# The first 336 columns of w_o as two loads of their own, one of them read in 5 groups of 16 rows

## The chip, the cores and the metric

The kernel runs on one core of one Trainium2 chip. The metric is the device time of one execution in microseconds (us), lower is better. The core has a matmul engine (PE), a vector engine (DVE), a scalar engine (ACT), a general one (POOL) and one that issues most transfers (SP). Transfers (DMAs) between the chip's memory (HBM) and the on-chip buffer (SBUF, 128 partitions) are carried out by 16 DMA engines, which are fed from queues: q1 holds what SP issues, q10 what ACT issues.

## What is computed

A decode step with one new token for each of two sequences. The input is normalised; one branch is attention over a cache of 4096 keys and values (16 query heads, 8 key heads, head size 256), followed by the output projection `wo`; the other is a small gated feed-forward. Cut to what matters:

```
xn = layernorm(x)                                  # 2 x 448
q  = xn @ wq                                       # 2 x 16 heads x 256
p  = softmax(q . k_cache / 16)                     # 4096 positions
o  = p . v_cache                                   # 2 x 16 x 256
s  = o.reshape(2, 4096) @ wo                       # wo: 4096 x 448
g  = silu(((xn @ w_gate) * (xn @ w_up)) @ w_down)
out = x + s * g
```

All data are float32. Nearly all bytes are the two caches (64 MB each) and the weights, 158.54 MB of reads, each read once.

## The kernel before

**Work and stages.** The 16 pairs of a key head and a sequence are taken one after the other. For each, PE multiplies the query with the keys (`scores`, tile `s`), DVE and ACT make the softmax, PE turns the weights (`turn`) and multiplies them with the values (`values`, tile `o`), and a few small instructions join the result into `oT`. Ahead of this stand the feed-forward and the query projection, behind it the output projection with `wo`.

**Transfers.** `dma_side` is the whole list of SP's loads in order: `wgu` in two pieces, `wd`, `wq`, then 16 steps of keys and values (`kv`, 8 MB each but for the first step, into the buffers `buf0` and `buf1` in turn), the values of the last two steps (`vv`, two loads of 4 MB), and `wo` in six loads. SP waits before a load only until the buffer it writes is free; so the loads stand in the queue well ahead of their start. ACT issues only two small loads, `x` (2 rows) and `xo` (8 rows).

**The output projection.** `wo` is laid out as 128 rows of 32 steps of 448 columns, one matmul step for each. `ABREAST = (14, 9, 4)` are the steps of the first three loads into the tile `low` (`early` = 27 steps), `DIRECT = (3, 1, 1)` those of the last three into the upper half of `buf1` (`late`). Each load has a semaphore of its own (`won`). In `pe_side`, the loop over `won` waits for a load and then does its steps: those of `low` are summed in four column groups of the tile `o` (`abreast`, line 322), which ACT then copies to `ys` and `spread` (line 326) adds to `acc`; those of `late` go into `acc` directly (line 446). After the last step DVE multiplies with the gate (line 295), adds `x` (line 298), and SP stores the result (line 140).

The part of `dma_side` that the change touches stands on lines 131 to 138; the matmul steps are on lines 433 to 456.

Of the kernel before, what the change touches and what calls it, by code (L numbers as in the profile page):

```python
# [8 lines left out]
B, D = 2, 448  # L9
# [15 lines left out]
WO = 4 * HKV  # L25
ABREAST = (14, 9, 4)
DIRECT = (3, 1, 1)


class Queue:  # L30
# [20 lines left out]
        self.e.wait_ge(sem, n).then_inc(sem, -n)  # L51


def program(nc, known, x, xo, wgu, wd, wq, kv, vv, wo, out):
    def sb(name, shape):
        return nc.alloc_sbuf_tensor(name, shape, F32).ap()

    def ps(name, shape):
        return nc.alloc_psum_tensor(name, shape, F32).ap()

    first = nc.alloc_semaphore("first")
    sems = {n: nc.alloc_semaphore(n) for n in (
        "x", "xg", "gu", "wd", "wq", "k0", "k1", "v14", "v15", "t0", "t1", "pt", "sr", "ob", "q", "m", "mx", "res")}
    won = [nc.alloc_semaphore(f"wo{i}") for i in range(len(ABREAST + DIRECT))]
    pe = Queue(nc, nc.tensor, "pe", known)
    dv = Queue(nc, nc.vector, "dv", known)
# [6 lines left out]
    low = sb("low", [128, 28 * FC])  # L73
# [7 lines left out]
    xg, gate, sig, r0, r1 = (sb(n, [128, SL]) for n in ("xg", "gate", "sig", "r0", "r1"))  # L81
# [8 lines left out]
    m = sb("m", [128, 2])  # L90
    mx = sb("mx", [1, NT, W])
    p = sb("p", [128, 2, 512])
    su = sb("su", [128, 2])
    sr = sb("sr", [128, 128])
    r = [sb(f"r{i}i", [128, REP]) for i in range(2)]
    pT = sb("pT", [128, 2, BLK, 128])
    ob = sb("ob", [128, 512])
# [4 lines left out]
    pt = [ps(f"pt{i}", [128, NK, 128]) for i in range(2)]  # L102
# [4 lines left out]
    late = buf[1][:, ROW:]  # L107
    bounds = [0]
    for n in ABREAST + DIRECT:
        bounds.append(bounds[-1] + n)  # L110
    early = bounds[len(ABREAST)]

    def wo_step(i):
        return low[:, i * D:(i + 1) * D] if i < early else late[:, (i - early) * D:(i - early + 1) * D]
# [4 lines left out]
    def dma_side():  # L119
        e = nc.sync  # L120
        for lo, hi in zip(GU, GU[1:]):
            e.dma_start(low[:, lo:hi], wgu[:, lo:hi]).then_inc(sems["gu"], 16)
        e.dma_start(buf[1][:, :14 * D], wd).then_inc(sems["wd"], 16)
        e.dma_start(buf[0][:, :28 * 512], wq).then_inc(sems["wq"], 16)
        sp.after(pe, "y4")
        for h in range(2):
            e.dma_start(buf[1][:, h * ROW:(h + 1) * ROW], kv[0][:, h * ROW:(h + 1) * ROW]).then_inc(sems[f"k{h}"], 16)
        for i in range(N - 2):
            sp.after(pe, *(("q", 1) if i == 0 else ("s", 1) if i == 1 else ("v", i - 2)))
            e.dma_start(buf[i % 2], kv[1 + i]).then_inc(turns[i % 2], 16)  # L130
        sp.after(pe, "v", N - 4)
        for h in range(2):
            e.dma_start(buf[0][:, h * ROW:(h + 1) * ROW], vv[h]).then_inc(sems[f"v{N - 2 + h}"], 16)
        for n, lo, hi in zip(won, bounds, bounds[1:]):
            if lo == early:
                sp.after(pe, "v", N - 3)
            t = low[:, lo * D:hi * D] if hi <= early else late[:, (lo - early) * D:(hi - early) * D]
            e.dma_start(t, wo[:, lo * D:hi * D]).then_inc(n, 16)
        sp.after(dv, "res")
        e.dma_start(out, r1).then_inc(sems["res"], 16)  # L140
        e.wait_ge(sems["res"], 16)
        last = nc.alloc_semaphore("last")
        e.sem_clear(range(first.num, last.num + 1))
# [156 lines left out]
    def pe_side():  # L300
        e = nc.tensor
# [18 lines left out]
        def abreast(t, lhs, rhs, i, total):  # L320
            c = i % NT
            return e.matmul(t[W * c:W * (c + 1), :D], lhs, rhs, start=i < NT, stop=i >= total - NT)  # L322

        def spread(start, stop):
            for c in range(NT):
                ins = e.matmul(acc[W * c:W * (c + 1), :SL], pick.rearrange("p b j -> p (b j)"),  # L326
                               ys[:, c * SL:(c + 1) * SL], start=start, stop=stop)
            return ins
# [77 lines left out]
        at, count = dict(pe.at), pe.n  # L406
# [26 lines left out]
        def left(i):  # L433
            g, j = divmod(i, 4)
            return oT[g][:, j // 2, j % 2].rearrange("p b j -> p (b j)")

        for n, lo, hi in zip(won, bounds, bounds[1:]):
            e.wait_ge(n, 16)
            for i in range(lo, hi):
                if i >= 4 * (HKV - 1):  # L440
                    pe.after(dv, "oT", N - 1)
                if i < early:
                    ins = abreast(o, left(i), wo_step(i), i, early)
                else:
                    for c in range(NT):
                        ins = e.matmul(acc[W * c:W * (c + 1), :SL], left(i), wo_step(i)[:, c * SL:(c + 1) * SL],  # L446
                                       start=lo == early and i == lo, stop=i == WO - 1)
            if hi == early:
                pe.ev(ins, "w4")
            if lo == early:  # L450
                pe.after(ac, "accs")
                spread(False, False)
# [3 lines left out]
    act_side()  # L456
    dve_side()
    dma_side()
    pe_side()
    return {q.name: q.at for q in (pe, dv, ac, po, sp)}  # L460

# [44 lines left out]
```

## Time and profile before

| | us |
|---|---|
| median of 3 runs | 375.0 (374.96 to 375.05) |
| the profiled execution, its own time | 375.17 |
| its span (first to last instruction of the profile) | 373.9 |

| engine | busy us | share of the span |
|---|---|---|
| PE, matmul | 243.6 | 65% |
| PE, weight load | 95.1 | 25% |
| DVE | 60.3 | 16% |
| ACT | 45.7 | 12% |
| POOL | 5.0 | 1% |
| q1 on the 16 DMA engines | | 98.4% |

The span starts with the first instruction in the profile; the own time also holds the start and the end around it, 1.3 us. The busy share of the DMA engines is a mean over 16: a share of 0.50 in a short stretch can mean that 8 of them are at work and 8 have run out.

### The profile page before, as it was taken

The numbers are of one execution on the slowest core, as the hardware profiler recorded it, in microseconds if no ns is written. First come the engines' busy times: TensorE is split into PE (matmuls) and PEld (weight loads), VectorE is DVE, ScalarE is ACT, GpSimd is POOL, SyncE is SP. The second block draws the span as 40 slices with busy tenths as digits, with TensorE's granted clock in tenths as the row PEclk, the third lists the DMA queues.
The fourth block names the chain that finished last, engine by engine and source line by source line (L and its number), as shares of the span: only waits on it lengthen the run. The fifth ranks groups of instructions, "written<-read, shape, count | busy, mean of one in ns | idle before, by whom it ended". The sixth has DMA issues, their size and how long they took to land. (4 is left out here: it accounts for less than half of the span.)

```text
span 373.9 us, 3749 instructions
## 1 busy us (share of the span) xinstructions
PE 243.6 (65%) x1642; PEld 95.1 (25%) x1642; DVE 60.3 (16%) x142; ACT 45.7 (12%) x105; POOL 5.0 (1%) x23
## 2 busy tenths in 40 slices
PE   0093295739393948585776767575758484849786
PEld 0021022322322222323231313122322222232332
DVE  3001002202121212112021203030302020202100
ACT  1002021010102020202020202020202010201110
POOL 1000000000000000000000000000000000000000
PEclk9998588758677687768596859596959586958899
DMA  9999999999999999999999999999999999999995
GB/s 369 400 459 413 430 424 438 444 444 449 449 429 400 435 429 435 449 442 436 407 435 435 435 442 435 449 428 414 435 428 442 442 442 442 400 417 435 417 421 211
DMA packets 4203, 158.70 MB, mean 424 GB/s; under 512 B 610, under 2 KB 868, under 8 KB 1252
## 3 DMA queue, kind: packets, MB, share of 16 engines
q1 hardware_dynamic: 4176, 158.59, 98.4%
q8 instruction: 5, 0.08, 0.1%
q14 instruction: 2, 0.02, 0.0%
q10 hardware_dynamic: 20, 0.01, 0.0%
HBM read 158.54 MB, written 0.06 MB: 424 GB/s over the span
## 5 line engine op out<-in xcount | busy, mean ns | idle before, releaser
L361 PE MATMUL s<-buf,qs 128*32 128x512 f32 x512 | 89.2, 860 | 58.1 <-PEq L51 58.1
L386 PE MATMUL o<-buf,pT 128*32 128x512 f32 x512 | 76.9, 610 | 0.3 <-DVE oT L272 0.3
L178 ACT ACTIVATE p<-s,m 128x512 f32<-128x512 f32 x32 | 21.7, 682 | 251.6 <-DVE m L253 251.6
L361 PEld LDWEIGHTS s<-buf,qs 128*32 128x32 f32 x512 | 22.5, 151 | 111.2 <-issue 111.1
L247 DVE TENSOR_REDUCE m<-s 128x1 f32<-128x1024 f32 x16 | 19.6, 1224 | 144.8 <-PE s L361 144.8
L317 PE MATMUL pt<-ident,p 128*128 128x128 f32 x128 | 22.2, 329 | 12.8 <-PEq L51 12.8
L394 PE MATMUL oc<-sel,ob 128*128 128x2 f32 x128 | 16.4, 250 | 19.8 <-PEq L51 19.8
L386 PEld LDWEIGHTS o<-buf,pT 128*32 128x32 f32 x512 | 17.1, 111 | 32.9 <-issue 30.6
L394 PEld LDWEIGHTS oc<-sel,ob 128*128 128x128 f32 x128 | 15.5, 191 | 33.9 <-issue 33.9
L317 PEld LDWEIGHTS pt<-ident,p 128*128 128x128 f32 x128 | 17.4, 166 | 13.7 <-issue 13.7
L308 PE MATMUL s<-buf,xnT 128*32 128x512 f32 x48 | 7.9, 813 | 10.8 <-DMA buf<-wq 10.8
L308 PE MATMUL s<-low,xnT 128*32 128x448 f32 x48 | 6.5, 692 | 11.9 <-DMA low<-wgu 11.9
L266 DVE COPY pT<-pt 128x512 f32<-128x512 f32 x16 | 11.1, 691 | 18.3 <-PE o L386 17.0
L249 DVE TENSOR_REDUCE mx<-sm 1x128 f32<-1x512 f32 x16 | 10.9, 679 | 10.1 <-PE sm L367 10.1
L192 ACT COPY ob<-o 128x512 f32<-128x512 f32 x16 | 9.3, 582 | 12.5 <-PE o L386 12.5
L183 ACT COPY pT<-pt 128x512 f32<-128x512 f32 x16 | 9.6, 601 | 2.4 <-PE pt L317 2.4
L371 PEld LDWEIGHTS sm<-one,mx 1*128 1x128 f32 x32 | 4.7, 183 | 13.8 <-issue 13.8
L158 POOL COPY qs<-qT 128x64 f32<-128x64 f32 x16 | 3.7, 236 | 293.8 <-PE s L361 243.1
L377 PEld LDWEIGHTS sm<-sel,sr 128*128 128x128 f32 x32 | 7.4, 288 | 0.0
L371 PE MATMUL sm<-one,mx 1*128 1x1 f32 x32 | 6.0, 255 | 1.7 <-PEq L51 1.7
L322 PE MATMUL o<-low,oT 128*32 128x448 f32 x54 | 6.4, 544 | 0.6 <-DMA low<-wo 0.6
L178 ACT ACTIVATION_READ_ACCUMULATOR p<-s,m 128x1 f32 x32 | 6.3, 196 | 0.0
(65 smaller groups left out, 62.4 us busy)
## 6 DMA issues: line engine op xcount, KB each, us to landing
buf<-kv SPq DMA_DIRECT2D x2, 4096.0 KB, 26.1
buf<-vv SPq DMA_DIRECT2D x2, 4096.0 KB, 23.1
buf<-wq SPq DMA_DIRECT2D x1, 7168.0 KB, 41.9
low<-wgu SPq DMA_DIRECT2D x1, 5824.0 KB, 17.0
buf<-wd SPq DMA_DIRECT2D x1, 3136.0 KB, 24.0
low<-wo SPq DMA_DIRECT2D x1, 3136.0 KB, 34.8
low<-wo SPq DMA_DIRECT2D x1, 2016.0 KB, 39.1
low<-wo SPq DMA_DIRECT2D x1, 896.0 KB, 40.9
```

The costliest lines, as they stand in the source:

```text
L178: ins = e.activation(p[:, h], s[:, h], AF.Exp, bias=m[:, 1:2], scale=1.0 / 16, accum_out=su[:, h:h + 1])
L183: e.copy(pT[:, 1], pt[1]).then_inc(sems["pt"], 1)
L192: e.copy(ob, o).then_inc(sems["ob"], 1)
L247: e.tensor_reduce(m[:, 0:1], s.rearrange("p h n -> p (h n)"), axis=AX.X, op=OP.max).then_inc(sems["m"], 1)
L249: e.tensor_reduce(mx, sm[:1, None, :128].rearrange("p o (c j) -> p o j c", c=NT).to_broadcast([1, NT, W, NT]), axis=AX.X, op=OP.max).then_ ...
L266: e.tensor_copy(pT[:, 0], pt[0]).then_inc(sems["pt"], 1)
L308: e.matmul(t[W * c:W * (c + 1), :n], xnT[:, k, :], block(NT * k + c), start=k == 0, stop=False)
L317: ins = e.transpose(t[:, i, :], a[:, i * 128:(i + 1) * 128], ident)
L361: ins = e.matmul(s[W * c:W * (c + 1), h], qs[i % 2][:, d].rearrange("p j q -> p (j q)"), k[:, h, d, c, :], start=d == 0, stop=d == 1)
L371: pe.ev(e.matmul(sm[:, 128:129], mx.rearrange("p c j -> p (c j)"), one, start=True, stop=True), "x", i)
L386: ins = e.matmul(o[W * at:W * (at + 1), :], pT[:, h, j, 64 * c + 16:64 * c + 48], v[:, h, j, c, :], start=h == 0 and j < 2, stop=h == 1 an ...
L394: ins = e.matmul(oc[:, 2 * d:2 * d + 2], ob[:, h * 256 + d * 128:h * 256 + (d + 1) * 128], sel[:, h], start=h == 0, stop=h == 1)
```

## The change

The first 336 of the first load's 6272 columns are taken out of it and loaded ahead of it in two loads, which share a new semaphore `lead`:

- rows 0 to 79 from a new input array `few`, a copy of that block of `wo` made on the host, stored as 5 groups of 17 rows of which 16 are read. The unused 17th row keeps the 5 groups apart in the access pattern: it is 5 x 16 x 336 in HBM, against 80 rows in SBUF.
- rows 80 to 127 from `wo`, 48 rows of 336 columns.

The first load of `wo` then begins at column 336 and is 128 rows of 5936 columns. Before the first step of the output projection PE waits for `lead` too. All bytes land where they landed before.

```diff
+LEAD = 3 * D // 4
+FEW = 5
...
-def program(nc, known, x, xo, wgu, wd, wq, kv, vv, wo, out):
+def program(nc, known, x, xo, wgu, wd, wq, kv, vv, few, wo, out):
...
         for h in range(2):
             e.dma_start(buf[0][:, h * ROW:(h + 1) * ROW], vv[h]).then_inc(sems[f"v{N - 2 + h}"], 16)
+        e.dma_start(low[:16 * FEW, :LEAD], few[:, :16]).then_inc(sems["lead"], 16)
+        e.dma_start(low[16 * FEW:, :LEAD], wo[16 * FEW:, :LEAD]).then_inc(sems["lead"], 16)
         for n, lo, hi in zip(won, bounds, bounds[1:]):
             if lo == early:
                 sp.after(pe, "v", N - 3)
-            t = low[:, lo * D:hi * D] if hi <= early else late[:, (lo - early) * D:(hi - early) * D]
-            e.dma_start(t, wo[:, lo * D:hi * D]).then_inc(n, 16)
+            if hi <= early:
+                at = max(lo * D, LEAD)
+                e.dma_start(low[:, at:hi * D], wo[:, at:hi * D]).then_inc(n, 16)
+            else:
+                e.dma_start(late[:, (lo - early) * D:(hi - early) * D], wo[:, lo * D:hi * D]).then_inc(n, 16)
...
+        e.wait_ge(sems["lead"], 2 * 16)
         for n, lo, hi in zip(won, bounds, bounds[1:]):
             e.wait_ge(n, 16)
...
+    few = np.zeros((FEW, 17, LEAD), wo.dtype)
+    few[:, :16] = wo[:16 * FEW, :LEAD].reshape(FEW, 16, LEAD)
```

On SP, from the last load of keys on, the list of the kernel before (a row: the line, the tile written and the tensor read, partitions x elements, how often):

```order
L130 DMA buf<-kv 128x16384 x14
L133 DMA buf<-vv 128x8192 x2
L138 DMA low<-wo 128x6272
L138 DMA low<-wo 128x4032
L138 DMA low<-wo 128x1792
L138 DMA buf<-wo 128x1344
L138 DMA buf<-wo 128x448 x2
L140 DMA res<-r 128x112
```

and that of the changed kernel, with its own line numbers:

```order
L132 DMA buf<-kv 128x16384 x14
L135 DMA buf<-vv 128x8192 x2
L136 DMA low<-few 80x1x336
L137 DMA low<-wo 48x336
L143 DMA low<-wo 128x5936
L143 DMA low<-wo 128x4032
L143 DMA low<-wo 128x1792
L145 DMA buf<-wo 128x1344
L145 DMA buf<-wo 128x448 x2
L147 DMA res<-r 128x112
```

Two loads stand between the values and the first of the long loads of `wo`, which is 336 columns narrower; nothing else on SP moved. On the other engines the instructions and their order are as they were, but for PE's one wait more.

## Rows read from the trace of the kernel before

**Rows 1.** Page, slices of the span: DMA engines' mean busy share in tenths; GB/s

```profile
DMA  9999999999999999999999999999999999999995
GB/s 369 400 459 413 430 424 438 444 444 449 449 429 400 435 429 435 449 442 436 407 435 435 435 442 435 449 428 414 435 428 442 442 442 442 400 417 435 417 421 211
```

**Rows 2.** Page, DMA queues: packets, MB, share of 16 engines' span

```profile
q1 hardware_dynamic: 4176, 158.59, 98.4%
q8 instruction: 5, 0.08, 0.1%
...
q10 hardware_dynamic: 20, 0.01, 0.0%
```

**Rows 3.** Chain that ended last, its end: start us, us, what

```profile
345.57 24.41 DMA buf<-wo
369.97 0.04 issue
370.01 0.78 PE acc L446 x24
370.80 0.19 PE acc L326 x8
370.99 0.58 PE acc L446 x16
...
371.59 0.28 DVE r L295
...
371.90 0.27 DVE r L298
```

**Rows 4.** Stretches of time: us, busy time by engine, PEclk, DMA share, GB/s

```profile
324.00:345.00 21.00, 14.87 (x97) 6.18 (x95) 3.50 (x8) 2.67 (x7) 0.00 (x0) 0.76 0.98 423
```

**Rows 5.** The same view for the end of the transfers, in half microseconds

```profile
368.00:368.50 0.50, 0.50 (x6) 0.10 (x8) 0.00 (x0) 0.00 (x0) 0.00 (x0) 1.00 1.00 384
368.50:369.00 0.50, 0.50 (x9) 0.06 (x8) 0.00 (x0) 0.00 (x0) 0.00 (x0) 1.00 0.71 272
369.00:369.50 0.50, 0.36 (x4) 0.00 (x0) 0.00 (x0) 0.07 (x1) 0.00 (x0) 1.00 0.43 168
369.50:370.00 0.50, 0.00 (x0) 0.00 (x0) 0.00 (x0) 0.46 (x1) 0.00 (x0) 1.00 0.36 136
370.00:370.50 0.50, 0.48 (x20) 0.49 (x24) 0.00 (x0) 0.00 (x0) 0.00 (x0) 1.00 0.23 86
370.50:371.00 0.50, 0.50 (x30) 0.44 (x20) 0.00 (x0) 0.00 (x0) 0.00 (x0) 1.00 0.02 7
```

**Rows 6.** DMA queues in the 2.4 us from 364.8: packets, MB, share of 16 engines

```profile
q1 hardware_dynamic: 164, 0.95, 96.3%
q8 instruction: 1, 0.02, 2.8%
```

**Rows 7.** Timeline, SP: issues of the last loads and of the store

```profile
325.66 0.80 SPq L133 DMA_DIRECT2D buf<-vv  x2
326.50 1.38 SPq L138 DMA_DIRECT2D low<-wo  x3
345.57 1.28 SPq L138 DMA_DIRECT2D buf<-wo  x3
372.20 0.35 SPq L140 DMA_DIRECT2D res<-r  x1
```

**Rows 8.** Page, DMA issues: KB, us from issue to landing

```profile
low<-wo SPq DMA_DIRECT2D x1, 3136.0 KB, 34.8
```

**Rows 9.** Timeline, PE in the output projection: start us, us, [idle before <-releaser]

```profile
362.36 3.20 PE L322 MATMUL o<-low,oT 128*32 128x448 f32 x28
...
366.13 0.16 PEld L322 LDWEIGHTS o<-low,oT 128*32 128x32 f32 x8 [1.37 <-DMA low<-wo]
...
370.01 0.54 PEld L446 LDWEIGHTS acc<-buf,oT 128*32 128x32 f32 x24 [1.46 <-DMA buf<-wo]
...
371.12 0.16 PEld L446 LDWEIGHTS acc<-buf,oT 128*32 128x32 f32 x8 [0.19 <-DMA buf<-wo]
```

More of the change, by code (lines that the diff above doesn't have):

```diff
@@ L62, in program @@
     sems = {n: nc.alloc_semaphore(n) for n in (
-        "x", "xg", "gu", "wd", "wq", "k0", "k1", "v14", "v15", "t0", "t1", "pt", "sr", "ob", "q", "m", "mx", "res")}
+        "x", "xg", "gu", "wd", "wq", "k0", "k1", "v14", "v15", "t0", "t1", "pt", "sr", "ob", "q", "m", "mx", "res", "lead")}
     won = [nc.alloc_semaphore(f"wo{i}") for i in range(len(ABREAST + DIRECT))]
@@ L491 @@
     wd = np.concatenate([full, last], 1).reshape(128, 14 * D)
-    arrays = dict(x=x, xo=xo, wgu=wgu, wd=wd, wq=wq, kv=kv, vv=vv, wo=wo)
+    arrays = dict(x=x, xo=xo, wgu=wgu, wd=wd, wq=wq, kv=kv, vv=vv, few=few, wo=wo)
     def build(known):
```

## Prediction

> **What bounds the kernel now.** I read the page's slices first. The 16 DMA engines are busy at nine tenths or more in every slice but the last, which is the end of the transfers [rows 1]; SP's queue alone holds them for 98.4% of the span [rows 2]. So the transfers set the time, and PE, busy 65%, waits for them. The chain that ended last says the same of the end: it runs back through two DVE instructions and the last matmuls into a transfer of `wo` that was issued at 345.57 and landed at 369.97 [rows 3]. A change of the loads moves the end if it moves the landing of the last ones, and by as much: of the last load PE's wait ends at 371.12, and from there to the end of the span, 373.9, lie the last matmuls, the two DVE instructions and the store [rows 3, 7, 9], which the change leaves alone.
>
> Then I read the end of the transfers in half microseconds [rows 5]. All engines are at work until 368.5. Then the share falls to 0.71, 0.43, 0.36, 0.23 and 0.02: times 16, that is about 11, 7, 6, 4 engines at work, and the last one stops near 370.6. The engines do not run out together. The sum of what is left after 368.5 is (0.71 + 0.43 + 0.36 + 0.23 + 0.02) x 0.5 = 0.88 us of all 16, so with perfect balance they would all stop at 369.4, 1.2 us earlier than the last does. That is the most that moving bytes between engines could gain. One reason for the difference can be seen: five transfers of instructions went through the same engines [rows 2], and one near the end took 2.8% of 16 x 2.4 us, 1.08 us of one engine [rows 6]. An engine that had one runs that much behind the others; there are five, and seven engines are still at work after 369.0.
>
> **The change part by part.** The bytes that land are the same. What changes is which engine carries how many, and in how many rows.
>
> How the rows are shared out: SP's 29 transfers (28 loads and the store) left 4176 packets, exactly 29 x (128 + 16), a packet for each row and one for each of 16 engines' completions; ACT's two loads of 2 and of 8 rows left 20, that is 2 + 2 and 8 + 8 [rows 2]. So the completions, and with them the engines, go by the count of the outermost groups, two for 2 and eight for 8. Five groups of 16 rows against 80 rows should then go to five engines with 16 rows each, and 48 rows to 16 engines with 3 each.
>
> The price of a row of 1344 bytes: in the long loads an engine moves 423 / (0.98 x 16) = 27.0 GB/s [rows 4]. In the stretch from 369.5, with rows of 1792 bytes, it is 136 / (0.36 x 16) = 23.6 GB/s, in the one before 168 / (0.43 x 16) = 24.4 [rows 5]; a row of 1792 takes 76 or 73 ns there, against 66 at the full rate, so each row costs 7 to 10 ns beside its bytes. I take 8, and 50 + 8 = 58 ns for a row of 1344 bytes.
>
> - The first long load loses 8 rows x 50 ns = 0.40 us on every engine (the same 8 rows remain, narrower).
> - The 48 rows add 3 x 58 = 0.17 us on every engine.
> - The 80 rows add 16 x 58 = 0.93 us on five engines.
>
> Eleven engines thus end 0.40 - 0.17 = 0.23 us earlier, five end 0.17 + 0.93 - 0.40 = 0.70 us later. With rows at 7 or 10 ns the first figure is 0.23 or 0.22, the second 0.69 or 0.74, and the further completions lie inside this.
>
> What this does to the end depends on when those five ended before. If the latest of them stopped 0.93 us or more ahead of the last engine, the end comes 0.23 us earlier; at 0.70 us ahead nothing changes; if one is the very last, the end comes 0.70 us later. No row says which engines the five are. Of 16, about seven stop after 369.0 and four after 370.0. Drawn blindly, five engines without any of the seven would be 126 of 4368, 3 in 100, and without any of the last four 792 of 4368, 18 in 100. But they are not drawn: I take the five that such a load gets, and those that carry instructions, to be fixed by some assignment, and the two may as well lie apart by it. I give 3 in 10 that they do. Otherwise the latest of the five is one of the four that stop in the last 0.6 us; I take 0.2 us ahead of the last, and the end comes 0.70 - 0.2 = 0.5 us later, between 0.1 and 0.70.
>
> The other parts cost nothing here. Two more issues on SP take about 0.43 us each, as the mean of the ones beside them [rows 7]; they put off the three loads of `wo` behind them to 327.4, and the first of those lands 34.8 us after its issue, since 8 MB of values and what is left of the last keys stand ahead of it [rows 8]. The wait ahead of the last three, until 345.57, covers the rest. Without that cover it would be 0.86 us. PE's new wait stands ahead of its first step at 362.36; the two lead loads stand in the queue ahead of the first long one, which lands at 361.3 (326.5 + 34.8), so PE finds both done, and even 1.5 us later would be taken up by the 1.37 us that PE waits for the second load [rows 8, 9]. Nothing else is queued on PE there that another engine waits for: ACT and DVE wait for the sum of all early steps.
>
> **The rivals.**
>
> *All five run early.* Then the end comes 0.23 us earlier: 375.0 - 0.2 = 374.8. For it: seven late engines leave nine. Against it: the count above.
>
> *The neighbours' path is shared.* Every SP load so far spans all 128 partitions (29 x 128 of the packets in [rows 2]), so that each engine may have a path into SBUF of its own, and 27.0 GB/s [rows 4] may be the path's rate as well as the engine's. The five engines now write 16 neighbouring rows each, into partitions that other engines are writing too, while all are busy (share 0.98 and 1.00 until 368.5 [rows 4, 5]). If two share a path, a row takes 2 x 50 + 8 = 108 ns, 16 take 1.73 us instead of 0.93, and the five end 1.5 us later; the 3 rows take 0.32 instead of 0.17, so the others gain 0.1 at most. With one of the last four among the five that is 0.5 + 0.8 = 1.3 us later: 376.3, between 375.8 and 376.9. With all five early (stopped by 368.5 to 369.0, some 1.6 to 2.1 us ahead of the last) the rest is about nothing: 375.0. It decides from the point at which an engine and its neighbours are both at work on the same partitions, so from the first lead row. For it: the rate is the same for all engines and does not vary between slices. Against it: no row shows two engines at work on the same partitions.
> [...]
>
> *The split is not by five.* If the 80 rows are spread over all 16 engines, each has 5 + 3 = 8 rows of 336 columns: 8 x 8 ns, 0.06 us later, 375.1, no change.
>
> **How the numbers follow.** The profiled execution took 375.17 us, of which 373.9 are its span; the median of the runs is 375.0, so 0.17 below. All terms are differences at the end of the transfers, so I put them on the median. Forecast: five engines get the 80 rows, one of the late ones among them, rates unchanged: 375.0 + 0.5 = 375.5, by itself 375.1 to 375.8, with the 0.1 us over which the runs spread. Chance 0.38. All five early, rates unchanged: 374.8, 0.22. Shared path with a late one: 376.3, 0.25; with all five early: 375.0, 0.08. No split by five: 375.1, 0.07.
>
> A measurement of this kernel can tell about 0.2% from no change, that is 0.75 us. Slower by more (over 375.75): the shared path with a late engine, 0.25, and the upper edge of the forecast, 0.04: 0.29. Faster by more (under 374.25) would take more than half of the 1.2 us that perfect balance could give, and no case here reaches it: 0.03. Within: 0.68. The range goes from the early case, 374.8 less that 0.1 us, to 376.5, which holds more than half of the shared path: 374.65 to 376.5. Outside is about 0.1 above, and little below.
>
> **What the profile after would show.** The split by five: SP's queue with 4176 + 80 + 5 + 48 + 16 = 4325 packets (16 in place of 5 if it is by sixteen). The five engines' extra work: DMA shares in the last half microseconds with a tail of up to five engines (0.31 or less) that lasts longer, or, in the early case, a steeper fall that ends 0.2 us earlier. The shared path: a stretch with shares near 1.00 at fewer GB/s than the 423 of before, where the lead loads run, around 353.7 (the 361.3 at which the first long load landed, less its 3.2 MB at 423 GB/s). The end: PE's wait before its last steps longer or shorter by the change of the time, and the 2.7 us from there to the end unchanged. The free parts: PE without a new wait at its first step. Wrong it would be if instructions were fetched at another place, or on another engine, than before; that moves an engine by about 1.1 us, as much as all terms here.

## The result, and the profile after

The changed kernel takes 375.9 us (median of 16 runs, 375.54 to 376.15), the kernel before 375.08 us (16 runs, 374.91 to 375.41). The ratio is 1.0021, interval 1.0014 to 1.0029: 0.8 us slower, between 0.5 and 1.1. The forecast was 375.5, by itself 375.1 to 375.8, with a range of 374.65 to 376.5. The measured time lies in the range, just above what the forecast gave by itself, and over 375.75, to which the prediction gave a chance of 0.29. The number held; its mechanism did not, as the runs below show.

The page of the changed kernel, DMA queues (packets, MB, share of 16 engines' span):

```profile
span 374.6 us, 3752 instructions
...
q1 hardware_dynamic: 4325, 158.59, 98.5%
```

4325 packets are 149 more than before [rows 2]: 80 rows with 5 completions, 48 rows with 16. So the 80 rows went to five engines, as the prediction had read it from the counts of other loads. The bytes are the same and the queue is as full as before.

The end of the transfers, in the stretches of half a microsecond that stand for before in [rows 5] (time, busy time by engine, PE clock, DMA share, GB/s):

```profile
369.00:369.50 0.50, 0.50 (x8) 0.21 (x8) 0.00 (x0) 0.00 (x0) 0.00 (x0) 1.00 0.95 366
369.50:370.00 0.50, 0.50 (x8) 0.00 (x0) 0.00 (x0) 0.00 (x0) 0.00 (x0) 1.00 0.69 265
370.00:370.50 0.50, 0.10 (x4) 0.00 (x0) 0.00 (x0) 0.36 (x1) 0.00 (x0) 1.00 0.57 215
370.50:371.00 0.50, 0.27 (x12) 0.27 (x16) 0.00 (x0) 0.17 (x1) 0.00 (x0) 1.00 0.37 140
371.00:371.50 0.50, 0.50 (x32) 0.50 (x24) 0.00 (x0) 0.00 (x0) 0.00 (x0) 1.00 0.05 18
```

The fall of the shares starts about a microsecond later (it began at 368.5 before, it begins at 369.5 now) and ends about 0.7 us later. It is not five engines alone that trail behind: the whole end of the transfers has moved back, the early engines included. Time must have been lost ahead of it, by all.

PE at the end (timeline; idle before, releaser), against [rows 9]:

```profile
362.18 3.20 PE L329 MATMUL o<-low,oT 128*32 128x448 f32 x28 [0.29 <-DMA low<-wo]
...
366.90 3.19 PE L329 MATMUL o<-low,oT 128*32 128x448 f32 x26 [1.53 <-DMA low<-wo]
...
371.83 0.16 PEld L454 LDWEIGHTS acc<-buf,oT 128*32 128x32 f32 x8 [0.18 <-DMA buf<-wo]
```

The last load is waited for until 371.83 instead of 371.12, 0.71 us longer, and the span is 0.7 us longer: the 2.8 us behind that wait are unchanged (the prediction calls them 2.7). At the first step PE now waits 0.29 us; it did not before, but the wait for the second load, until 366.90, comes behind it and takes that up.

Where the 0.7 us went shows in one stretch, the 8 us around the place where the two lead loads run. The kernel before, and then the changed kernel, each with the stretch ahead of it and the one behind (the view counts a row whole in the stretch in which it starts, so a share can pass 1.00):

```profile
346.00:350.00 4.00, 2.59 (x22) 2.49 (x26) 0.84 (x4) 1.15 (x4) 0.00 (x0) 0.91 0.97 418
350.00:358.00 8.00, 6.88 (x52) 2.33 (x48) 0.93 (x3) 1.07 (x2) 0.00 (x0) 0.83 0.99 424
358.00:366.00 8.00, 6.76 (x64) 2.40 (x52) 0.23 (x1) 0.58 (x1) 0.00 (x0) 1.00 0.98 412
```

```profile
346.00:350.00 4.00, 3.13 (x22) 2.84 (x26) 0.59 (x3) 0.61 (x2) 0.00 (x0) 0.80 0.95 410
350.00:358.00 8.00, 6.88 (x56) 2.38 (x52) 0.92 (x2) 1.07 (x2) 0.00 (x0) 0.89 1.01 384
358.00:366.00 8.00, 6.29 (x56) 2.46 (x48) 0.22 (x1) 0.58 (x1) 0.00 (x0) 1.00 0.97 408
```

All engines are busy (share 1.01), and yet they move 384 GB/s instead of 424. The bytes missing are 8 us x 40 GB/s = 320 KB, at 424 GB/s 0.75 us: the whole loss. Ahead of the stretch and behind it the rate is within 2% of that before (410 and 408 against 418 and 412). This is the sign that the prediction named for the shared path, at the place that it named.

### The profile page after: what moved, and what is told of

Read it like the earlier page. It is cut to its first block, busy times and chain, and to the rows that moved or that the text cites. A ratio compares the mean times of both kernels' runs of the same rounds, so it can differ in the third digit from the quotient of the medians.

```text
span 374.6 us, 3752 instructions
## 1 busy us (share of the span) xinstructions
PE 246.5 (66%) x1642; PEld 95.4 (25%) x1642; DVE 60.4 (16%) x142; ACT 45.7 (12%) x105; POOL 5.0 (1%) x23
## 3 DMA queue, kind: packets, MB, share of 16 engines
q1 hardware_dynamic: 4325, 158.59, 98.5%
## 5 line engine op out<-in xcount | busy, mean ns | idle before, releaser
L368 PE MATMUL s<-buf,qs 128*32 128x512 f32 x512 | 90.8, 873 | 57.7 <-PEq L53 57.7
```

The lines of the kernel that those rows point to most:

```text
L368: ins = e.matmul(s[W * c:W * (c + 1), h], qs[i % 2][:, d].rearrange("p j q -> p (j q)"), k[:, h, d, c, :], start=d == 0, stop=d == 1)
```

## The experiments

Two theories stood against each other. **A**: engines don't hinder each other, and one of the late ones was among the five that got 80 rows (the forecast). **B**: engines that write into partitions which other engines write share a path with them (the rival). A third, **C**, came with the run over all 128 rows: more loads and shorter rows cost the time, wherever they go.

**The first load in two halves of rows.** Same engines, same bytes, other partitions at one time.

```diff
-            e.dma_start(t, wo[:, lo * D:hi * D]).then_inc(n, 16)
+            if lo == 0:
+                for r in (slice(0, 64), slice(64, 128)):
+                    e.dma_start(t[r], wo[r, :hi * D]).then_inc(n, 16)
+            else:
+                e.dma_start(t, wo[:, lo * D:hi * D]).then_inc(n, 16)
...
-            e.wait_ge(n, 16)
+            e.wait_ge(n, 32 if lo == 0 else 16)
```

> The kernel before, with its first load of w_o (3.2 MB) issued as two loads of 64 rows, rows 0 to 63 and rows 64 to 127; each of the 16 engines then carries 4 + 4 rows of the same length, as many bytes as before. Theory A (the five engines that got the 80 rows had a late one among them; engines do not hinder each other): no change, within 0.1 us. Theory B (engines that write into neighbouring partitions share a path): 64 neighbouring rows reach only half of the paths, so the 3.2 MB go at about half of 424 GB/s: 7.6 us more, at least 3 us if the engines are out of step.

Measured: 385.52 us, ratio 1.0279 (1.0263 to 1.0294), 10.5 us slower. Its stretches of 4 us:

```profile
352.00:356.00 4.00, 3.50 (x24) 0.70 (x16) 0.43 (x1) 0.43 (x1) 0.00 (x0) 0.76 0.73 115
356.00:360.00 4.00, 3.38 (x32) 1.77 (x36) 0.49 (x2) 0.65 (x2) 0.00 (x0) 1.00 1.01 213
360.00:364.00 4.00, 2.31 (x20) 1.10 (x12) 0.23 (x1) 0.58 (x1) 0.00 (x0) 1.00 1.16 251
364.00:368.00 4.00, 0.00 (x0) 0.00 (x0) 0.00 (x0) 0.00 (x0) 0.00 (x0) 0.52 0.89 185
368.00:372.00 4.00, 0.00 (x0) 0.00 (x0) 0.00 (x0) 0.00 (x0) 0.00 (x0) 0.50 0.87 231
372.00:376.00 4.00, 3.92 (x24) 1.17 (x26) 0.00 (x0) 0.00 (x0) 0.00 (x0) 0.50 0.96 407
```

The engines are at work nearly all of the time (a mean share of 0.93), and move 199 GB/s in the mean of the five stretches until the halves are through, then 407. Single stretches swing about that mean, because a row of the halves takes 1.4 to 2.8 us and counts where it starts. Here 64 of the 128 partitions took 199 of 424 GB/s, about half of the rate, though by the mean share of 0.93 nearly all of the 16 engines were at work. Theory A, no change, is out. The loss is larger than the 7.6 us of a plain halving, and the rows in the trace tell where the rest is: the rows of the halves took 134 us of engine time beyond the 931 ns that such a row takes before, the last rows of values ahead of them 11 us beyond the shortest, and the rows of the load behind them 24 us. Together that is 169 us, 10.6 us for each of 16 engines: the halves also slow the loads ahead and behind, which are in flight beside them.

**The same 80 rows over 16 engines.**

```diff
-        e.dma_start(low[:16 * FEW, :LEAD], few[:, :16]).then_inc(sems["lead"], 16)
+        e.dma_start(low[:16 * FEW, :LEAD], wo[:16 * FEW, :LEAD]).then_inc(sems["lead"], 16)
```

> The changed kernel, with its 80 rows read straight from w_o instead of 5 groups of 16: they go to 16 engines, 5 rows each, and with the 48 rows each engine has 8 again. Theory A: 8 more rows of 8 ns each, 0.06 us more than before, no change. Theory B: nobody has more bytes, but the 8 rows still go to partitions that others write: between 0.1 and 0.5 us slower than before, less than the changed kernel's 0.8.

Measured: 375.83 us, ratio 1.0021 (1.0012 to 1.0030), as slow as the changed kernel. The same 8 us:

```profile
350.00:358.00 8.00, 6.88 (x48) 2.26 (x50) 1.06 (x3) 1.07 (x2) 0.00 (x0) 0.80 0.99 379
```

SP's queue now has 4336 packets, 16 completions for each of the two loads. Nobody carries more bytes here, and the loss is all there: 45 GB/s over 8 us, 0.85 us at 424. So the imbalance of five against eleven is not needed for it. Under B the guess of 0.1 to 0.5 us was too small.

**The first 336 columns over all 128 rows.** The changed kernel, without the load of 80 rows, and with the other one over all rows:

```diff
-        e.dma_start(low[:16 * FEW, :LEAD], few[:, :16]).then_inc(sems["lead"], 16)
-        e.dma_start(low[16 * FEW:, :LEAD], wo[16 * FEW:, :LEAD]).then_inc(sems["lead"], 16)
+        e.dma_start(low[:, :LEAD], wo[:, :LEAD]).then_inc(sems["lead"], 16)
...
-        e.wait_ge(sems["lead"], 2 * 16)
+        e.wait_ge(sems["lead"], 16)
```

> The changed kernel with its first 336 columns as one load over all 128 rows, so that every engine writes its usual partitions, 8 rows more of 1344 bytes. Theory B (shared paths make the whole loss): 0.06 us slower than before, no change. Theory C (the loss comes from more loads and shorter rows as such, whatever partitions they go to): 0.4 to 0.8 us slower.

Measured: 375.18 us against 375.14, ratio 1.0001 (0.9992 to 1.0010): no change.

```profile
350.00:358.00 8.00, 6.88 (x56) 2.36 (x52) 0.92 (x2) 1.07 (x2) 0.00 (x0) 0.87 0.99 421
```

The same columns as rows of the same length cost nothing here (421 GB/s against 424) when one load spans all 128 partitions, as the long loads do. So theory C is out: it is not the shorter rows, nor a load more. Nor is it where the bytes are read, as this run and the one over 16 engines read the same rows of `wo` in the same pieces. What is left is where they go: 421 GB/s in one load over 128 rows, 379 in loads of 80 and of 48.

**More bytes for five engines, into their own partitions and apart.** Both runs add loads into a spare tile that nobody reads to the kernel before, 53.8 KB for each of five engines, the first into partitions 0 to 19 and 32 to 51 (called the five's own here and in the tables below), the second into 0 to 79; PE waits for their landing as it waits for the lead loads. (The lines that make the tile, the array and the semaphore are left out of the edits here and below.) The first:

```diff
+        e.dma_start(spare[0:20], few[0, :, :4]).then_inc(sems["lead"], 16)
+        e.dma_start(spare[32:52], few[1, :, :4]).then_inc(sems["lead"], 16)
         for n, lo, hi in zip(won, bounds, bounds[1:]):
```

> The kernel before, and ahead of the loads of w_o two more loads into a spare tile that nobody reads: 5 groups of 4 rows into partitions 0 to 19 and 5 groups of 4 rows into partitions 32 to 51, 6720 bytes a row. Five engines get 8 rows each, 2.06 us of work more (53.8 KB at 27.0 GB/s and 8 ns a row), into the partitions which, by the order of rows in the loads over 128 partitions, they write in all other loads as well. Theory A: a late engine is among the five, at most 0.2 us ahead of the last: 1.9 to 2.1 us slower. Theory B: the five stop some 0.9 us ahead of the last, and here no path is shared: 1.1 to 1.3 us slower.

the second:

```diff
+        e.dma_start(spare[:80, :840], few[:, :16]).then_inc(sems["lead"], 16)
         for n, lo, hi in zip(won, bounds, bounds[1:]):
```

> As the run with 5 groups of 4 rows, with the same bytes for the same five engines, but as 5 groups of 16 rows of 3360 bytes into partitions 0 to 79: 2.12 us of work more on five engines if nothing hinders them. Theory A: as the run with groups of 4 rows, within 0.1 us. Theory B: each engine writes partitions that other engines write at that time; rows take up to twice as long, 1.0 to 2.0 us slower than the run with groups of 4 rows.

Measured: 376.44 us, ratio 1.0036 (1.0022 to 1.0049), 1.35 us slower; and 378.89 us, 1.0103 (1.0088 to 1.0119), 3.9 us slower. The 8 us of the one and of the other:

```profile
350.00:358.00 8.00, 6.88 (x52) 2.33 (x48) 0.92 (x2) 1.07 (x2) 0.00 (x0) 0.83 1.00 428
```

```profile
350.00:358.00 8.00, 6.88 (x60) 2.44 (x56) 0.92 (x2) 1.07 (x2) 0.00 (x0) 0.93 1.01 323
```

The same bytes for five engines: 428 GB/s with the extra rows in partitions 0 to 19 and 32 to 51, 323 with them in 0 to 79. The 2.5 us between the runs, more than the 1.0 to 2.0 expected, is the price of the place, all but 0.06 us that the further rows of the second cost by the estimates. The first run also tells how much the five have in hand: 2.06 us of work moved the end by 1.35, a little more than theory B's 1.1 to 1.3, so the latest of them stops about 0.7 us ahead of the last engine (0.2 to 1.2 by the interval). That 0 to 19 and 32 to 51 are what the five write in the loads over 128 rows, as I had taken for the first run, is borne out by the rate alone (428 GB/s, against 424 in the kernel before); which engine writes which partitions, no trace names.

Single rows in the traces say the same. From the packets of five kernels, of the loads around the place, from about 344 us on ("columns" is the run over all 128 rows; ns; the last column is the sum over all rows of what each took beyond the shortest):

```
kernel                 row bytes  rows  shortest  median  longest  sum beyond, us
before                    25088   128       931     934      944             0.5
columns, 128 rows          1344   128        58      58       60             0.0
columns, 128 rows         23744   128       882     888      904             0.9
changed kernel             1344   128        58      75      108             2.2
changed kernel            23744   128       885     888     1271             8.3
changed kernel            32768   101      1213    1218     1769             3.0
five, own partitions       6720    40       255     265      274             0.4
five, apart                3360    80       132     221      295             6.7
five, apart               25088   128       931     939     1889            22.6
```

In the changed kernel the lead rows take 58 ns at the shortest, as forecast, and up to 108, the figure of the rival. But the larger sum, 8.3 us, is with the long rows behind them. With 3.0 us of the same kind on the last rows of values it makes 13.5 us of engine time, by 16 engines 0.84 us each (in the run over all 128 rows the three sums are 0.0, 0.9 and 0.4).

The trace names no engine for a row and no partition, but the rows can be told apart by engine. In these traces each row starts 3 to 22 ns before the one ahead of it on its engine has ended, without a gap, and each engine has a fixed number of rows of every load; so the rows from 344 us on fall into 16 chains. Where each chain ends its last row of `wo` (us; extra rows are those of the 80 rows, or of the spare tile; the last three kernels follow below):

```
kernel                 engines without extra rows   engines with extra rows
before                 16: 368.28 to 370.65
changed kernel         11: 369.29 to 371.02         370.18 370.32 370.41 370.96 371.36
80 rows over 16        16: 369.29 to 371.48
five, own partitions   11: 368.67 to 370.44         370.77 371.18 371.39 371.88 371.94
eight, own partitions   8: 368.83 to 370.59         370.55 370.62 370.83 371.09 371.86 371.91 372.46 372.47
four times, five       11: 371.72 to 373.81         375.14 375.21 375.38 376.23 376.51
four times, 16         16: 371.65 to 373.53
```

In the run into own partitions the extra rows took 2.1 us on each of the five. Without them the five would end between about 368.6 and 369.8, the latest 0.6 us ahead of the last of the others: three of them are early, two lie in the middle, and none is among the last. In the kernel before, where the last seven engines end at 369.52, 369.78, 370.13, 370.34, 370.43, 370.56 and 370.65, that fits the engine of 369.78 as the latest of the five, 0.87 us ahead of the last. In the changed kernel the engine that ends last, at 371.36, is one of the five. Its rows took 0.9 us more than undisturbed ones: 0.4 on its last seven rows of values, 0.4 on its 19 lead rows and 0.1 on its long rows. The other eleven lose too, and their last ends 0.4 us later than the last engine did before.

**More bytes for eight engines.** The run into own partitions, with 8 groups of 4 rows instead of 5.

```diff
-        e.dma_start(spare[0:20], few[0, :, :4]).then_inc(sems["lead"], 16)
-        e.dma_start(spare[32:52], few[1, :, :4]).then_inc(sems["lead"], 16)
+        e.dma_start(spare[0:32], few[0, :, :4]).then_inc(sems["lead"], 16)
+        e.dma_start(spare[32:64], few[1, :, :4]).then_inc(sems["lead"], 16)
```

> As the run with 5 groups of 4 rows into the engines' own partitions (1.35 us slower than before), but 8 groups of 4 rows, into partitions 0 to 31 and 32 to 63: eight engines get the same 2.06 us of work more. If the engines that end last (some that carried instructions) are among the three added ones, the end moves by nearly all of it, 1.8 to 2.1 us; that would make the five early ones, some 0.7 us ahead of the last. If a late one was among the five already, the same 1.35 us again.

Measured: 377.05 us, ratio 1.0060 (1.0044 to 1.0075), 2.25 us slower (1.9 by the medians). Nearly all of the 2.06 us reaches the end: among the three engines added is one of those that end last. The intervals of the two runs just overlap (1.0049 and 1.0044), so the times alone make this likely rather than certain; the chains show it, as two of the eight end at 372.46 and 372.47, more than 0.5 us behind the other six.

**One of the two loads alone, four times as wide.** A load more into the spare tile, 48 rows into partitions 80 to 127, or 80 rows into partitions 0 to 79, 1344 columns each.

```diff
+        e.dma_start(spare[80:, :1344], few).then_inc(sems["lead"], 16)
```

> The kernel before with one more load into a spare tile that nobody reads: 48 rows into partitions 80 to 127, as in the change but four times as wide (5376 bytes a row), 3 rows for each of 16 engines: 3 x 207 ns, 0.62 us of work more on every engine. Without shared paths: 0.6 us slower. With them: more, by 48 of 128 parts of four times the changed kernel's loss of 0.8 us, 0.6 + 1.2 = 1.8 us slower, if both loads of the change lose alike per row.

```diff
+        e.dma_start(spare[:80, :1344], few).then_inc(sems["lead"], 16)
```

> As the run with 48 rows, with 80 rows into partitions 0 to 79, four times as wide as in the change, over 16 engines: 5 x 207 ns, 1.03 us of work more on every engine. Without shared paths: 1.0 us slower. With them: by 80 of 128 parts, 1.0 + 2.0 = 3.0 us slower.

Measured: 377.62 us, ratio 1.0067 (1.0052 to 1.0083), 2.5 us slower, where the bytes alone would cost 0.6; and 378.40 us, 1.0089 (1.0074 to 1.0105), 3.3 us, where they would cost 1.0. So both lose, 1.9 and 2.3 us; the plain 48 rows, which I had priced as harmless, seem to lose more per row than the 80 (0.04 against 0.03 us, though the intervals of the two overlap).

**Four times as wide, over five engines and over 16.** The changed kernel, and the run with 16 engines, with

```diff
-LEAD = 3 * D // 4
+LEAD = 3 * D
```

> The changed kernel with 1344 columns instead of 336 in the two loads ahead. The shared paths lose per byte: four times 0.8 us, 3.2 us. The imbalance: five engines have 16 + 3 rows of 207 ns more and 8 x 199 ns less, 2.3 us of work more, of which they have 0.7 us in hand. If the imbalance counts beside the shared paths once it is larger than what the five have in hand, 4.0 to 5.0 us slower than before, and more than the run over 16 engines by 0.8 us or more; if only the paths count, both alike.

> The same with 1344 columns, the 80 rows over 16 engines (5 rows each) instead of five: no imbalance. The shared paths alone, four times the 0.8 us measured at 336 columns: 3.2 us slower than before.

Measured: 381.81 us, ratio 1.0182 (1.0165 to 1.0199), 6.8 us slower, over five engines, more than the 4.0 to 5.0 expected; 378.21 us, 1.0078 (1.0061 to 1.0095), 2.9 us, over 16. By theory B the second is the shared paths alone, roughly in proportion to the bytes (2.9 us where 3.2 were expected). The first shows the imbalance, which at 336 columns puts the last of the five only 0.3 us behind the other engines: the end of the transfers of that run has few engines trailing far behind.

```profile
373.00:374.00 1.00, 1.00 (x13) 0.25 (x6) 0.00 (x0) 0.00 (x0) 0.00 (x0) 1.00 0.45 183
374.00:375.00 1.00, 1.00 (x10) 0.25 (x8) 0.00 (x0) 0.00 (x0) 0.00 (x0) 1.00 0.33 131
```

A share of 0.33 is about five engines of 16; by the chains it is the five, which end 1.3 to 2.7 us behind the last of the other eleven. The imbalance by itself, 2.3 us less the 0.7 in hand, would give 1.6 of the 3.6 us between the medians of the two runs. The rest may come from the 16 of the 80 rows that each of the five has, where each of the 16 has 5: the 19 lead rows of the engine that ends last took 8.3 us, where undisturbed rows take 3.9. No run separates the two.

## Why the prediction was right, and where it was wrong

- **What bounds the kernel, and the end.** Right: the loss is in the transfers, and the last landing and the span moved by the same 0.7 us, with what lies behind them unchanged.
- **How rows go to engines.** Right: 4325 packets. The price of a row, 58 ns, is what an undisturbed row took (58 in both traces). The price of a transfer of instructions, 1.08 us, was too low: by its chain, the engine that had one at 365.2 in the kernel before ended 1.5 us later than its rows around 352 would have put it.
- **Which five.** Wrong: I forecast that the latest of the five is one of the four that stop last, 0.2 us ahead of the last. It is none of them, and has 0.6 to 0.9 us in hand by the times and the chains, about what I had worked out as the extra work of the five. By the forecast's own sum, with that in hand and rates unchanged, the end would hardly have moved.
- **Rates unchanged.** This is the step that failed. The engine that ends last has the 0.70 us of extra work that was forecast and 0.9 us of slow rows besides, which take it to 371.36, from 369.78 if that was its place before. The forecast's 0.5 us was 0.70 less the 0.2 in hand; the runs show 0.70 and 0.9 less 0.87, that is 0.7. Two errors of similar size, a slack that was too small and slow rows that were left out, offset each other. That the number came close is luck.
- **The rival of the shared path.** The sign that it forecast is there: 384, 379 and 323 GB/s at shares of 1.01, 0.99 and 1.01, where the kernel before has 424 at 0.99. That a shared path is the cause is still theory B's account, as no trace shows a path. Its price for the five came close, in part by luck: it put them 1.5 us later (1.65 by its own terms, 1.73 + 0.32 - 0.40), and the last of them ends about 1.6 us later, but its 19 lead rows took 1.47 us, not 2.05, and 0.4 us came from rows of values. Neither of its two cases was right, a late engine among the five (376.3) or all five early (375.0), as the five lie between. And I had let only the five engines' 16 rows and the 3 rows of the others become longer. Two things were missing: rows of other loads beside them, of `wo` and of the values, are slowed down as well (8.3 and 3.0 of 13.5 us in the table above), so that all engines lose; and the 48 rows lose of themselves (1.9 us beyond their bytes when four times as wide). The term "the others gain 0.1 at most" should have been a loss: 0.4 us in the changed kernel, and in the run over 16 engines, where no five are, the whole 0.8.
- **Free parts.** SP's two issues took 0.91 and 0.40 us, not 0.43 each, and cost nothing, as they were issued more than 20 us ahead of 351.5, where the first lead row starts (timeline of SP, changed kernel):

```profile
327.66 0.91 SPq L136 DMA_DIRECT2D low<-few  x1
328.62 0.40 SPq L137 DMA_DIRECT2D low<-wo  x1
```

  PE's 0.29 us at its first step is a wait for the first long load, which landed at 362.1; the lead rows had been through since 354.4, so the new wait cost nothing, as forecast.
- **No split by five**: out, by the packets.

No run showed a version that beats the kernel before. By theory B the loads over 128 rows already give every path the same bytes; moving rows to another engine leaves the bytes of a path as they are and makes two engines meet on it. This, and that it holds for every such shift, is argued from the rates of these runs (424 and 421 GB/s with loads over 128 rows alone, 384 and 379 with those of 80 and 48 rows), not shown.

## What to carry to other kernels

When transfers bound a kernel, a rebalancing of DMA engines has to be looked at twice: how many bytes each engine carries, and into which partitions it writes. A load over fewer than 128 partitions beside other loads can slow the others down, as here by 8.3 us of engine time on the long rows of `wo` and 3.0 on those of values, and the rate in a stretch with every engine busy (384 GB/s at a share of 1.01, where the kernel before has 424) is the place to see it. Following the rows engine by engine then tells which engine ends last, and on which rows it lost the time. A slack found in the end of a transfer is worth only what the rows that the shift slows down leave of it (here 0.9 us of slow rows, against 0.87 in hand), and a run that adds bytes to the supposed early engines, in partitions where they cost no rate (428 GB/s here), measures that slack directly.

## What was not expected of the hardware

Two loads of 64 rows in place of one of 128 cost 10.5 us for 3.2 MB. And 48 rows of 1344 bytes over all 16 engines, the most harmless-looking part of the change, lose when four times as wide 1.9 us beyond their bytes: neither few engines nor much data (48 x 5376 bytes, 258 KB) was needed for a loss here.
